# Expert-weight loads issued from a GpSimd copy beside the first row gather, the first rows turned three steps later, and eight weight subtractions on GpSimd

## The chip, the cores and the metric

One core of one Trainium2 chip runs the whole program. The metric is the device time of one execution in microseconds (us), as the median of several executions. The engines are TensorE (PE: matmul and transpose), VectorE (DVE), ScalarE (ACT), GpSimd (POOL) and SyncE (SP, which here only issues transfers). Each runs its own instructions in their order, and they wait for each other by semaphores.

## The reference

Three stages follow each other: attention within clusters, a dense feed-forward layer (FFN), and a layer of eight experts with one chosen expert per token.

```python
x = attention(q, k, v, centroids)                 # (1536 tokens, 512)
h = np.maximum(x @ w_in, 0.0)                     # 512 x 2048
x = h * h @ w_out                                 # 2048 x 512
do_compute = x @ w_skip > 0
e_idx = np.argmax(x[do_compute] @ w_gate, axis=1) # 8 experts
out = x.copy()
for e in range(8):
    mask = e_idx == e
    h = np.maximum(xc[mask] @ w1[e], 0.0)         # 512 x 1024
    y[mask] = gate_w[mask, None] * (h @ w2[e])    # 1024 x 512
out[do_compute] = xc + y
```

All data are fp32. The change lies where the FFN hands over to the experts.

## The kernel before

Every fp32 product is made of three matmuls on a split of each operand: a high part (names that end in `h`, fp32r, rounded by a cast on ACT) and a low part (names that end in `l`, the difference, subtracted on DVE or GpSimd).

**The FFN** works on four chunks of 384 tokens in four passes over the hidden width; its last matmuls add into `acc` (L1087), and `x` of a block of 128 tokens is complete when DVE has added the last pass (L1095). Each block is then stored twice, to the scratch `xd` (L815) and to the output `out` (L816); the last chunk's stores go out on ACT's queue. `turn_x` transposes it too (L819, copied by ACT to `xs`, L821) for the routing products `lps` (L825).

**The routing** counts how many tokens want each expert, gives each its rank within its expert, and makes lists of rows. The fullest expert gets two lists: A, its first 128 tokens, which can be known before the last chunk is routed, and B, the next ones; the other seven experts have one each. `choose()` finds the fullest expert and writes its number and that of the next to `pi`. `place(n)` reads expert numbers from `pi` into registers of SP, and `fetch()` issues the loads of weights: pieces of 512 KB, as many as there are free staging buffers (five at first: three `st` and two of the `xc` tiles that aren't needed any more), and again whenever one comes free. `half_weights` consumes a piece: ACT casts it (`wih`, `woh`, L761), two subtractions of 128x512 make the low part (`wil`, `wol`, L765). The tables `ENG0` to `ENG2` say on which engines, `a` for ACT, `v` for DVE and `p` for GpSimd, with eight entries for the eight pieces of an expert (four of w1, four of w2); `ENG1` is for the second expert in the order.

**The expert units** are numbered u = 0 to 8: units 0 and 1 are lists A and B with the weights of the fullest expert, unit u from 2 on is expert u - 1 in the order. `gather(u)` fetches the rows of a list with an indirect transfer from GpSimd's queue (L1017), the first one from `out`, the others from `xd`. `parts()` transposes the rows (`xps`, L1025), ACT casts them (`xh`, or `hh` for the hidden values, L1028), DVE subtracts (`xl`, `hl`, L1029). `g1` makes the hidden products `hps`, `g2` the products `acc` (both L1035), `turn_h` transposes the hidden values, and `finish` scales the rows, adds them (`yo`, L1056) and scatters them to `out` (L1058). `between(gen, f)` runs `f` behind the second of the four groups of three matmuls of a product, so that the transposes and what follows on ACT and DVE lie beside the rest.

**The order.** The last steps of the FFN and unit 0 form one stream of steps on TensorE, `base()`. At the step numbers of the table `EVENTS` other work is put in: `e` the next part of the routing up to the third chunk (`early()`), `l` that of the last chunk (`late()`), `c` one piece of expert weights, `x` the transposes of list A (`x_of_A`). TensorE's order in this stretch is written by hand in that way; on ACT, DVE and GpSimd a scheduler orders the instructions by priority and readiness, and each engine then runs its list strictly in order. Behind the stream comes a loop over the units 1 to 8.

Of the kernel before, what the change touches and what calls it, by code (L numbers as in the profile page):

```python
# [7 lines left out]
F32 = mybir.dt.float32  # L8
F32R = mybir.dt.float32r
BF16 = mybir.dt.bfloat16  # L10
I32 = mybir.dt.int32
AF = mybir.ActivationFunctionType
ALU = mybir.AluOpType
# [23 lines left out]
PE, ACT, DVE, POOL, SP = (mybir.EngineType.PE, mybir.EngineType.Activation, mybir.EngineType.DVE,  # L37
                          mybir.EngineType.Pool, mybir.EngineType.SP)
EVENTS = ((1, 'e'), (2, 'e'), (3, 'e'), (4, 'e'), (8, 'e'), (11, 'e'), (12, 'c'), (13, 'e'), (15, 'c'),
          (16, 'cce'), (18, 'el'), (21, 'x'), (22, 'lcc'), (25, 'c'), (26, 'l'), (28, 'lc'), (30, 'l'), (34, 'll'))  # L40
ENG0 = ('av',) * 8
ENG1 = ('av',) * 8
ENG2 = ('av',) * 8
HOLD = 2
M0 = {DVE, PE, ACT, POOL}
AFTER = 0
PACE = 3
# [5 lines left out]
def clustered_attention_moe(  # L53
# [16 lines left out]
    nc = tc.nc  # L70
# [4 lines left out]
    E, _, F2 = w1.shape  # L75
# [24 lines left out]
    inner = ExitStack()  # L100
    inner.enter_context(tc.manual_schedule(engines=M0))
    nc.vector.memset(slot, 1.0)
# [30 lines left out]
    def do(gen):  # L133
        for _ in gen:
            pass
# [130 lines left out]
    with ExitStack() as actx:  # L266
# [417 lines left out]
        for i in range(-LA, NQ + GT + 1):  # L684
            if i == CLOSE:
                inner.close()
            for op in ORDER.split():
                op, lag = op.rstrip("'"), op.count("'")
# [13 lines left out]
    rp = ctx.enter_context(tc.tile_pool(name="rp", bufs=1, reuse_waits="tile"))  # L702
# [24 lines left out]
    loads = [h + (c,) for h in halves for c in (0, 2)]  # L727
    ENGS = [ENG0, ENG1] + [ENG2] * E

# [5 lines left out]
    def stage(t):  # L735
        free.append(t[:, 0:1024].rearrange("p (c f) -> p c f", c=2))

    def fetch():

        while free and loads and loads[0][0] < len(e_reg):  # L740
            p, kind, n, c = loads.pop(0)
            st = free.pop(0)
            nc.sync.dma_start(out=st, in_=w_slice(e_reg[p], kind, n)[:, c:c + 2])
            loaded.append(st)
# [39 lines left out]
    def econvert_to(units):  # L784
        while edone[0] < min(units, len(halves)):
            if next(egen) == "unit":
                edone[0] += 1
# [16 lines left out]
    ixp, pi = [rp.tile([128, E], I32, name=nm) for nm in ("ixp", "pi")]  # L804
# [97 lines left out]
    def ranks(ch, base=None):  # L902

        sbs = [128, GT, 128]
        rk = rank[:, ch * GT:ch * GT + GT]
        if base is not None:
            rkb = rp.tile([128, GT, 1], F32, name="rkb", bufs=2)
            nc.vector.tensor_scalar(out=rkb, in0=rk, scalar1=base, scalar2=None, op0=ALU.subtract)
            rk = rkb
        so = rp.tile(sbs, BF16, name="so", bufs=2)  # L910
        nc.vector.tensor_tensor(out=so, in0=slot.rearrange("p (o s) -> p o s", o=1).to_broadcast(sbs),
                                in1=rk.to_broadcast(sbs), op=ALU.is_equal)
        return so

    def slots(ch, sum, so):

        sl = ps_l.tile([128, 5, E], F32, name="sl", tag="l")
        for i in range(GT):
            nc.tensor.matmul(out=sl.rearrange("p a e -> p (a e)"), lhsT=so[:, i],
                             rhs=pay[:, ch * GT + i].rearrange("p a e -> p (a e)"),  # L920
                             start=(i == 0), stop=(i == GT - 1))
        if ch == 0:
            nc.vector.tensor_copy(out=sum[:, 0:5], in_=sl)
        else:
            nc.vector.tensor_tensor(out=sum[:, 0:5], in0=sl, in1=sum[:, 0:5], op=ALU.add)
# [7 lines left out]
    def choose():  # L933

        nc.vector.tensor_reduce(out=cmax, in_=cnt, op=ALU.max, axis=AX.X)
        nc.vector.tensor_scalar(out=full, in0=cnt, scalar1=cmax, scalar2=None, op0=ALU.is_equal)
        nc.vector.tensor_tensor(out=full, in0=full, in1=rev8[:, 0], op=ALU.mult)
        er = rp.tile([128, 1], F32, name="er")
        nc.vector.tensor_reduce(out=er, in_=full, op=ALU.max, axis=AX.X)
        nc.vector.tensor_scalar(out=full, in0=full, scalar1=er, scalar2=None, op0=ALU.is_equal)  # L940
        nc.vector.tensor_scalar(out=pi[:, 0:1], in0=er, scalar1=-1.0, scalar2=float(E), op0=ALU.mult, op1=ALU.add)
        nc.vector.tensor_scalar(out=pi[:, 1:2], in0=full[:, 1:2], scalar1=-1.0, scalar2=1.0,
                                op0=ALU.mult, op1=ALU.add)
        nc.vector.tensor_scalar_min(nA, cmax, 128.0)
        place(2)

    def place(n):
        while len(e_reg) < n:
            p = len(e_reg)
            e_reg.append(nc.sync.value_load(pi[0:1, p:p + 1], min_val=0, max_val=E - 1))  # L950
            if p == 0:
                fetch()

    def pick(i, sum):

        nc.vector.tensor_tensor(out=t2[:, 0:5], in0=sum[:, 0:5], in1=fullb[:, 0:5], op=ALU.mult)
        nc.vector.tensor_reduce(out=sAB[i][:, 0:5], in_=t2[:, 0:5], op=ALU.add, axis=AX.X)
        index(ixAB[i], sAB[i][:, 5:6], sAB[i].rearrange("p (a e) -> p a e", e=1))
        lists[i] = (ixAB[i], sAB[i][:, 5:6])

    def early():

        for ch in range(NC - 1):
            while done[0] <= ch:
                yield
            yield from route(ch)
            so = ranks(ch)
            yield
            if ch == NC - 2:
                choose()  # L970
            slots(ch, sg, so)
            if ch == NC - 2:
                pick(0, sg)
                gather(0)
            if ch < HOLD:
                stage(xc[ch])
            if ch == NC - 2:
                so = ranks(0, nA)
            yield
        for ch in range(NC - 1):  # L980
            slots(ch, sgB, so)
            if ch < NC - 2:
                so = ranks(ch + 1, nA)
            yield

    def late():
        yield from route(NC - 1)
        so, so2 = ranks(NC - 1, nA), ranks(NC - 1)
        yield
        slots(NC - 1, sgB, so)  # L990
        pick(1, sgB)
        gather(1)
        for ch in range(HOLD, NC):
            stage(xc[ch])
        yield
        slots(NC - 1, sg, so2)
        nc.vector.tensor_tensor(out=sgp, in0=sg[:, :, 0:1].to_broadcast([128, 6, E]), in1=sg, op=ALU.subtract)
        nc.vector.tensor_tensor(out=sgp, in0=sgp, in1=fullb, op=ALU.mult)
        nc.vector.tensor_tensor(out=sgp, in0=sgp, in1=sg, op=ALU.add)
        index(ixp, gp, sgp)  # L1000
        for p in range(1, E):
            lists[p + 1] = (ixp[:, p:p + 1], gp[:, p:p + 1])
        gather(2)
        nc.vector.tensor_copy(out=pi, in_=sgp[:, 5])
        place(E)
        yield


    UN = E + 1
# [3 lines left out]
    def gather(u):  # L1013

        xg = xgs[u % 3]
        nc.gpsimd.memset(xg, 0.0)
        nc.gpsimd.indirect_dma_start(  # L1017
            out=xg, in_=xd if u else out, in_offset=bass.IndirectOffsetOnAxis(ap=lists[u][0], axis=0),
            out_offset=None, bounds_check=N - 1, oob_is_err=False)

    def parts(src, name):

        tps = ps_x.tile([128, 4, 128], F32, name="xps", tag="x")
        for c in range(4):
            nc.tensor.transpose(out=tps[:, c], in_=src[:, c * 128:(c + 1) * 128], identity=ident)  # L1025
        hh = ep.tile([128, 4, 128], F32R, name=name + "h")
        hl = ep.tile([128, 4, 128], F32R, name=name + "l")
        nc.scalar.copy(out=hh, in_=tps)  # L1028
        nc.vector.tensor_tensor(out=hl, in0=tps, in1=hh.bitcast(F32), op=ALU.subtract)  # L1029
        return hh, hl  # L1030

    def products(ps, x, w, start, stop):
# [13 lines left out]
    def turn_h(u, n):  # L1046
        hp_t[u, n] = parts(hs_t.pop((u, n)), "h")

    def g2(u, n):
        if n == 0:  # L1050
            y_t[u] = ps_o.tile([128, DM], F32, name="acc")
        yield from products(y_t[u], hp_t.pop((u, n)), hexp[max(u - 1, 0), 1, n], n == 0, n == FB - 1)
# [45 lines left out]

    LG = 2
    bg = early()  # L1100
    lead = len(steps) - NF
    s2 = 0
# [40 lines left out]
    def between(gen, f):  # L1143
        for i, _ in enumerate(gen):
            if i == 1:
                f()
            yield
# [8 lines left out]
    n = 0  # L1156
# [22 lines left out]
    for u in range(1, UN):  # L1179
        econvert_to(4 * u)  # L1180
        do(g1(u, 0))
        if u > 1:
            do(g2(u - 1, 1))
            finish(u - 1)
            turn_h(u, 0)
        if u + 2 < UN:
            gather(u + 2)
        econvert_to(4 * u + 2)
        do(g1(u, 1) if u > 1 else between(g1(u, 1), lambda: turn_h(u, 0)))
        if u + 1 < UN:  # L1190
            xp_t[u + 1] = parts(xgs[(u + 1) % 3], "x")
        do(g2(u, 0))
        turn_h(u, 1)
    do(g2(UN - 1, 1))
    finish(UN - 1)

# [65 lines left out]
```

## Time and profile before

| what | us |
|---|---|
| median of 3 executions | 688.0 (686.8 to 688.48) |
| the profiled execution | 688.21 |
| its span, first to last instruction | 686.5 |
| TensorE busy | 655.3 (95%) |
| VectorE busy | 481.0 (70%) |
| ScalarE busy | 415.1 (60%) |
| GpSimd busy | 253.0 (37%) |
| mean granted TensorE clock | 0.984 of full |

The span leaves 1.7 us of the profiled execution outside. Times in rows count from the start of the span. The FFN ends near 555 us, routing and unit 0 lie between 540 and 575, and from there to 678 TensorE works through the units 1 to 8. A busy share is a mean over all stages, so the stretch around the change is read by itself, in rows in order of time.

### The profile page before, as it was taken

To read this page: it belongs to the slowest core of one execution; us is meant where nothing else is said; L and a number is where in the kernel's file an instruction comes from. 1 tells how busy PE (TensorE), PEld (TensorE's weight loads), DVE (VectorE), ACT (ScalarE), POOL (GpSimd) and SP (SyncE) were. 2 spreads that over 40 slices of the span, in tenths; PEclk is the share of its full clock that TensorE was granted. 3 is DMA by queue.
4 is the path that set the end of the run, shared out by engine and by line. 5 is a ranking of instruction groups with operands and counts; after the bars stand their busy time and mean duration, and the time that the engine had idled before them with its cause. 6 is when DMAs were issued, how large, how long until landed. Compare 5 with 4: busy or idle time off the path is not lost. (4 is left out here: it accounts for less than half of the span.)

```text
span 686.5 us, 11273 instructions
## 1 busy us (share of the span) xinstructions
PE 655.3 (95%) x3769; PEld 569.2 (83%) x3769; DVE 481.0 (70%) x928; ACT 415.1 (60%) x846; POOL 253.0 (37%) x329
## 2 busy tenths in 40 slices
PE   7889999999999999899999999999999898999994
PEld 6688988988888888889899999999888676888883
DVE  5678999999999999664365656522244688899950
ACT  6779989989998986444433333322232275778830
POOL 4534555536365445644344453421110203113110
PEclk9999999999999999999999999999999989999998
DMA  6567565655655200213212222101222596999900
GB/s 138 144 163 198 136 160 134 149 139 137 149 122 126 55 13 1 69 62 103 67 63 77 69 71 91 40 0 47 93 91 82 177 336 243 369 361 362 364 14 23
DMA packets 72034, 89.90 MB, mean 131 GB/s; under 512 B 32384, under 2 KB 43584, under 8 KB 71968
## 3 DMA queue, kind: packets, MB, share of 16 engines
q1 hardware_dynamic: 69664, 84.52, 41.7%
q0 software_dynamic: 1440, 3.01, 1.2%
q10 hardware_dynamic: 864, 1.57, 0.6%
q8 instruction: 32, 0.52, 0.3%
q14 instruction: 34, 0.28, 0.1%
HBM read 62.18 MB, written 9.44 MB: 104 GB/s over the span
## 5 line engine op out<-in xcount | busy, mean ns | idle before, releaser
L580 DVE TENSOR_TENSOR pl<-pt,ph 128x384 fp32r<-128x384 f32 x192 | 103.5, 550 | 19.8 <-ACT ph L571 18.3
L259 ACT ACTIVATE r<-hps 128x384 f32<-128x384 f32 x62 | 30.4, 491 | 125.8 <-PE hps L252 120.6
L557 PE MATMUL pt<-ident,p 128*128 128x128 f32 x576 | 97.1, 279 | 4.7 <-DVE pl L580 3.7
L515 PE MATMUL sc<-B,A 80*128 80x384 f32 (+1 forms) x384 | 93.4, 364 | 4.5 <-DMA A<-hi 1.8
L571 ACT CAST ph<-pt 128x384 fp32r<-128x384 f32 x192 | 89.7, 480 | 10.5 <-PE pt L557 9.7
L522 DVE TENSOR_REDUCE nm<-sc 128x1 f32<-128x768 f32 x96 | 90.9, 947 | 3.5 <-PE sc L515 3.4
L262 DVE TENSOR_TENSOR hl<-r,hh 128x384 fp32r<-128x384 f32 x62 | 37.4, 604 | 77.0 <-POOL hh L138 77.0
L531 ACT ACTIVATE p<-sc,nm 128x768 f32<-128x768 f32 x96 | 87.3, 909 | 6.0 <-DVE nm L522 5.5
L557 PEld LDWEIGHTS pt<-ident,p 128*128 128x128 f32 x576 | 70.8, 142 | 20.2 <-DVE pl L580 13.1
L138 POOL TENSOR_SCALAR hh<-r 128x384 fp32r<-128x384 f32 x62 | 36.5, 589 | 137.9 <-ACT r L260 118.8
L1087 PE MATMUL acc<-woh,hh 128*128 128x512 f32 x186 | 74.6, 401 | 0.0
L1087 PE MATMUL acc<-woh,hl 128*128 128x512 f32 x186 | 73.9, 397 | 0.0
L1087 PE MATMUL acc<-wol,hh 128*128 128x512 f32 x186 | 73.9, 397 | 0.0
L590 PE MATMUL av<-ph,vs 128*128 128x384 f32 x192 | 73.4, 382 | 0.1
L515 PEld LDWEIGHTS sc<-B,A 80*128 80x128 f32 (+1 forms) x384 | 63.9, 193 | 9.6 <-ACT p L531 5.3
L590 PE MATMUL av<-pl,vs 128*128 128x384 f32 x192 | 65.7, 342 | 0.6 <-DVE pl L580 0.6
L252 PE MATMUL hps<-A,wil 128*128 128x384 f32 x184 | 62.1, 338 | 1.8 <-POOL wil L184 1.8
L252 PE MATMUL hps<-A,wih 128*128 128x384 f32 x184 | 62.5, 340 | 0.0
L252 PE MATMUL hps<-B,wih 128*128 128x384 f32 x184 | 62.1, 337 | 0.0
L1087 PEld LDWEIGHTS acc<-woh,hl 128*128 128x128 f32 x186 | 35.3, 190 | 8.0
L1087 PEld LDWEIGHTS acc<-woh,hh 128*128 128x128 f32 x186 | 35.2, 190 | 5.8 <-DVE xc L1095 0.2
L1087 PEld LDWEIGHTS acc<-wol,hh 128*128 128x128 f32 x186 | 35.3, 190 | 5.3
(260 smaller groups left out, 1474.6 us busy)
## 6 DMA issues: line engine op xcount, KB each, us to landing
xc<-in_moe_w_dram SPq DMA_DIRECT2D x34, 512.0 KB, 5.8
st<-in_moe_w_dram SPq DMA_DIRECT2D x30, 512.0 KB, 5.7
st<-in_moe_w_in_dram SPq DMA_DIRECT2D x64, 128.0 KB, 2.9
st<-in_moe_w_out_dram SPq DMA_DIRECT2D x16, 512.0 KB, 3.5
A<-hi SPq DMA_DIRECT2D x30, 192.0 KB, 3.1
B<-hi SPq DMA_DIRECT2D x30, 192.0 KB, 3.1
qn<-in_q_dram SPq DMA_DIRECT2D x16, 192.0 KB, 3.3
kn<-in_k_dram SPq DMA_DIRECT2D x16, 192.0 KB, 3.6
```

The source lines that it names most:

```text
L138: nc.gpsimd.tensor_scalar(out=o, in0=i, scalar1=1.0, scalar2=0.0, op0=ALU.mult, op1=ALU.add)
L252: nc.tensor.matmul(out=hps, lhsT=wi[w][:, c, f * 128:(f + 1) * 128], rhs=xhl[ch][a][:, c], start=(n == 0), stop=(n == 3 * KD - 1))
L259: nc.scalar.activation(out=r, in_=hps, func=AF.Relu)
L262: nc.vector.tensor_tensor(out=hl, in0=r, in1=hh.bitcast(F32), op=ALU.subtract)
L515: nc.tensor.matmul(out=sc[:, c, 0:384], lhsT=A[h][0:kk, a, t * 128:(t + 1) * 128], rhs=Bk[h][0:kk, a, c * 384:(c + 1) * 384], start=(a == ...
L522: nc.vector.tensor_reduce(out=nm_t[i], in_=sc_t[i][:, :, 0:384], op=ALU.max, axis=AX.XY, negate=True)
L531: nc.scalar.activation(out=p, in_=sc[:, :, 0:384], func=AF.Exp, bias=nm, scale=1.0, accum_out=su_t[n, c][:, t, h:h + 1])
L557: nc.tensor.transpose(out=pt[:, c], in_=p_t[i][:, n, c * 128:(c + 1) * 128], identity=ident)
L571: nc.scalar.copy(out=block(i, n)[by_pool].bitcast(F32) if by_pool else block(i, n)[0], in_=pt_t[i, n])
L580: nc.vector.tensor_tensor(out=pl, in0=pt_t.pop((i, n)), in1=ph.bitcast(F32), op=ALU.subtract)
L590: nc.tensor.matmul(out=av, lhsT=vs[:, c, 2 * h:2 * h + 2].rearrange("p x d -> p (x d)"), rhs=r[:, c], start=(c == 0 and i == 0), stop=(c = ...
L1087: nc.tensor.matmul(out=acc, lhsT=h2[a][:, i * 128:(i + 1) * 128], rhs=wo[w][:, f], start=(f == 0 and n == 0), stop=(f == NF - 1 and n == 2))
```

## The change

Five edits:

- The event `x` (transposes of list A) moves from step 21 to step 24.
- The first four pieces (w1) of the second expert in the order have their low parts subtracted on GpSimd instead of DVE: eight instructions of 128x512.
- `choose()` no longer calls `place(2)`. Behind `gather(0)` in the program's text a GpSimd copy of two numbers, `first2`, is made, and `place` reads from that, so that SP's first register load, and behind it the first five weight loads, wait for this copy.
- In `parts()` the cast and the subtraction get a higher priority in the scheduler (`AHEAD`).
- In the last unit the transposes of the second half of the hidden values are put between the groups of the first half's product, as units 0 and 1 have it already.

```diff
-          (16, 'cce'), (18, 'el'), (21, 'x'), (22, 'lcc'), (25, 'c'), (26, 'l'), (28, 'lc'), (30, 'l'), (34, 'll'))
+          (16, 'cce'), (18, 'el'), (22, 'lcc'), (24, 'x'), (25, 'c'), (26, 'l'), (28, 'lc'), (30, 'l'), (34, 'll'))
-ENG1 = ('av',) * 8
+ENG1 = ('ap',) * 4 + ('av',) * 4
+AHEAD = 120
...
         nc.vector.tensor_scalar_min(nA, cmax, 128.0)
-        place(2)
-
-    def place(n):
+
+    def place(n, pi):
...
                 gather(0)
+
+                first2 = rp.tile([128, 2], I32, name="first2")
+                nc.gpsimd.tensor_copy(out=first2, in_=pi[:, 0:2])
+                place(2, first2)
...
-        place(E)
+        place(E, pi)
...
-        nc.scalar.copy(out=hh, in_=tps)
-        nc.vector.tensor_tensor(out=hl, in0=tps, in1=hh.bitcast(F32), op=ALU.subtract)
+        with tc.high_priority(offset=AHEAD):
+            nc.scalar.copy(out=hh, in_=tps)
+            nc.vector.tensor_tensor(out=hl, in0=tps, in1=hh.bitcast(F32), op=ALU.subtract)
...
-        do(g2(u, 0))
-        turn_h(u, 1)
+        if u + 1 < UN:
+            do(g2(u, 0))
+            turn_h(u, 1)
+        else:
+            do(between(g2(u, 0), lambda: turn_h(u, 1)))
```

The lines of the changed kernel are one to eight numbers higher: the gather is L1021, the copy L977, the subtractions L766, the casts L762, the out store L817, `xs` L822, `parts()` L1029 and L1033, the products L1040.

GpSimd, from the FFN's last high parts `hh` to the gathers of list A (index `ixA`), list B (`ixB`) and unit 2 (`ixp`). Before:

```order
L138 TENSOR_SCALAR hh<-r 128x384 x21
L1017 DMA u<-out_dram,ixA 128x512
L1017 DMA u<-xd,ixB 128x512
L1017 DMA l_5821<-xd,ixp 128x512
L1058 DMA out_dram<-yo,ixA 1536x512
```

With the change:

```order
L139 TENSOR_SCALAR hh<-r 128x384 x20
L977 COPY first_6541<-pi 128x2
L139 TENSOR_SCALAR hh<-r 128x384
L1021 DMA u<-out_dram,ixA 128x512
L766 TENSOR_TENSOR wil<-xc_91,wih 128x512 x2
L766 TENSOR_TENSOR wil<-xc_92,wih 128x512 x2
L766 TENSOR_TENSOR wil<-st,wih 128x512 x4
L1021 DMA u<-xd,ixB 128x512
L1021 DMA l_5821<-xd,ixp 128x512
```

The copy stands ahead of the gather of list A, with one `hh` between them, and the eight subtractions stand ahead of the gather of list B.

ACT, from the last chunk's first stores to the first cast of `woh` (`xc_94` are blocks of `x`; `xh` is the cast of list A). Before:

```order
L815 DMA xd<-xc_94 128x512
L761 CAST wih<-st 128x1024
L816 DMA out_dram<-xc_94 128x512
L761 CAST wih<-st 128x1024
L821 COPY xs<-xps 128x512
L761 CAST wih<-st 128x1024
L1028 CAST xh<-xps 128x512
L761 CAST wih<-xc_91 128x1024
L815 DMA xd<-xc_94 128x512
L816 DMA out_dram<-xc_94 128x512
L821 COPY xs<-xps 128x512
L761 CAST woh<-xc_92 128x1024
```

With the change:

```order
L816 DMA xd<-xc_94 128x512
L817 DMA out_dram<-xc_94 128x512
L762 CAST wih<-st 128x1024 x2
L822 COPY xs<-xps 128x512
L816 DMA xd<-xc_94 128x512
L762 CAST wih<-st 128x1024
L762 CAST wih<-xc_91 128x1024
L1033 CAST xh<-xps 128x512
L817 DMA out_dram<-xc_94 128x512
L822 COPY xs<-xps 128x512
L762 CAST woh<-xc_92 128x1024
```

The first cast of weights has moved behind the first store to `out`, the copy `xs` stands behind two casts as it did, and `xh` behind four.

TensorE, from the FFN's last products to the first hidden product of unit 0. Before:

```order
L1087 MATMUL acc<-woh,hl 128x512
L1025 MATMUL xps<-ident,u 128x128 x4
L1087 MATMUL acc<-woh,hh 128x512
L1087 MATMUL acc<-wol,hh 128x512
L1087 MATMUL acc<-woh,hl 128x512
L819 MATMUL xps<-ident,xc_94 128x128 x4
L825 MATMUL lps<-wgs,xs 128x9 x4
```

With the change:

```order
L1092 MATMUL acc<-woh,hl 128x512
L820 MATMUL xps<-ident,xc_94 128x128 x4
L826 MATMUL lps<-wgs,xs 128x9 x4
L1092 MATMUL acc<-woh,hh 128x512
L1092 MATMUL acc<-wol,hh 128x512
L1092 MATMUL acc<-woh,hl 128x512
L1092 MATMUL acc<-woh,hh 128x512
L1092 MATMUL acc<-wol,hh 128x512
L1092 MATMUL acc<-woh,hl 128x512
L1029 MATMUL xps<-ident,u 128x128 x4
L1040 MATMUL hps<-wih,xh 128x512
```

The transposes of list A (`u`) have moved behind the routing's transposes, its products and the last six products of the FFN, and stand now right ahead of unit 0.

## Rows read from the trace of the kernel before

**Rows 1.** Stretches: us; busy (instructions) of PE, PEld, DVE, ACT, POOL; PEclk; DMA share; GB/s.

```profile
545.50:548.20 2.70, 0.09 (x2) 0.01 (x1) 0.50 (x1) 0.00 (x0) 0.00 (x0) 1.00 1.00 369
548.20:555.40 7.20, 7.01 (x26) 5.67 (x27) 4.39 (x7) 6.29 (x8) 0.00 (x0) 0.55 1.03 385
...
566.00:569.30 3.30, 1.64 (x13) 1.11 (x13) 3.30 (x12) 2.46 (x4) 0.00 (x0) 1.00 0.91 325
569.30:572.70 3.40, 3.40 (x9) 2.62 (x9) 3.40 (x16) 2.59 (x4) 2.30 (x2) 0.51 0.56 203
...
577.00:673.50 96.50, 96.38 (x461) 78.44 (x462) 81.07 (x138) 66.12 (x86) 17.59 (x20) 1.00 0.79 286
```

**Rows 2.** TensorE's waits from 530 to 686 us: total, times, longest.

```profile
PE xps L1025 <- DMA u<-out_dram,ixA: 2.6, 1, 2.6
PE sl L919 <- DVE pay L896: 1.7, 2, 1.1
```

**Rows 3.** In order of time, SP: start, us, instruction, count.

```profile
539.51 1.66 SPq L743 DMA_DIRECT2D st<-in_moe_w_dram  x3
541.41 0.98 SPq L743 DMA_DIRECT2D xc<-in_moe_w_dram  x2
545.53 0.38 SPq L743 DMA_DIRECT2D st<-in_moe_w_dram  x1
```

**Rows 4.** In order of time, GpSimd: in brackets the idle time before and its releaser.

```profile
540.58 1.56 POOL L1017 DMA_INDIRECT u<-out_dram,ixA  x1 [0.62 <-DVE hl L262]
570.09 1.38 POOL L1017 DMA_INDIRECT u<-xd,ixB  x1 [27.95 <-DMA xc<-in_moe_w_dram]
```

**Rows 5.** The tile ixA (gather 0 and a later scatter).

```profile
DMA to landing us min/median/max: 7.6/7.7/7.8
```

**Rows 6.** The tile ixB (gather 1 and a later scatter).

```profile
DMA to landing us min/median/max: 3.6/4.2/4.9
```

**Rows 7.** In order of time, DVE, routing of the last chunk.

```profile
562.96 0.69 DVE L765 TENSOR_TENSOR wil<-xc,wih 128x512 fp32r<-128x512 f32 x1
...
569.66 0.15 DVE L929 SCALAR_TENSOR_TENSOR ixB<-sB 128x1 int32<-128x1 f32 x1
```

**Rows 8.** In order of time, TensorE, from gather 0 to list B.

```profile
551.08 1.71 PE L825 MATMUL lps<-wgs,xs 128*128 128x9 f32 x8
...
555.35 0.58 PE L1035 MATMUL hps<-wih,xh 128*128 128x512 f32 x1
...
574.62 0.60 PE L1025 MATMUL xps<-ident,u 128*128 128x128 f32 x4
```

**Rows 9.** In order of time, TensorE, the last two units.

```profile
661.25 0.60 PE L1025 MATMUL xps<-ident,hs 128*128 128x128 f32 x4
661.60 0.48 PE L1035 MATMUL hps<-wih,xh 128*128 128x512 f32 x1
...
673.27 0.60 PE L1025 MATMUL xps<-ident,hs 128*128 128x128 f32 x4
674.54 0.51 PE L1035 MATMUL acc<-woh,hh 128*128 128x512 f32 x1 [0.68 <-ACT hh L1028]
...
675.27 0.50 PE L1035 MATMUL acc<-woh,hl 128*128 128x512 f32 x1
```

**Rows 10.** In order of time, ACT.

```profile
543.03 1.05 ACT L761 CAST wih<-st 128x1024 fp32r<-128x1024 f32 x1 [3.66 <-DMA st<-in_moe_w_dram]
...
548.59 1.05 ACT L761 CAST wih<-st 128x1024 fp32r<-128x1024 f32 x1 [4.51 <-DMA u<-out_dram,ixA]
549.54 0.58 ACT L821 COPY xs<-xps 128x512 f32<-128x512 f32 x1
...
561.40 1.03 ACT L761 CAST wih<-xc 128x1024 fp32r<-128x1024 f32 x1
```

**Rows 11.** Line 184, GpSimd: count, duration ns min/median/max, first and last start.

```profile
L184 POOL TENSOR_TENSOR wil<-u,wih x16: 1277/1390/1715, 102.1 to 436.4; 128x512 fp32r<-128x512 f32 x16
L184 POOL TENSOR_TENSOR wol<-u,woh x16: 1273/1296/1607, 131.6 to 446.4; 128x512 fp32r<-128x512 f32 x16
```

## The prediction

> **What bounds the kernel now.** I read the page, a table of stretches, TensorE's waits, and the instructions in order of time. The page gives TensorE 95% of the span (the table above has its busy time); from 577.00 to 673.50 us it is busy 96.38 of 96.50 us at full clock [rows 1], so a microsecond gained or lost in front of 577 reaches the end. What can still move lies where the FFN hands over to the expert units, and behind 673.5. Three places:
>
> First, gather 0 (list A): issued at 540.58, landed 7.6 us later, and TensorE waits 2.6 us for it [rows 2, 4, 5]. After that stop the clock is 0.55 over 7.20 us [rows 1], which costs 7.20 x 0.45 = 3.2 us of matmul time. The five 512 KB weight loads that SP issued from 539.51 on are in flight beside it [rows 3], and DMA is full [rows 1]; their being the reason of the 7.6 us is an inference.
>
> Second, routing. From 566.00 to 569.30 TensorE works 1.64 of 3.30 us, mostly waiting for DVE's `pay` (1.7 us of the waits), then runs 3.40 us at clock 0.51, a loss of 1.7 us [rows 1, 2]. Gather 1 (list B) goes out at 570.09, 0.4 us after its index, on a GpSimd that had been idle for 27.95 us, and its rows land 3.6 us later [rows 4, 6, 7] (the larger figures of rows 6 and 7 belong to a later scatter with the same index; 570.09 + 4.9 would be past its reader). B's transposes start at 574.62 with no wait before them [rows 8]: gather 1 has under 1 us of slack (570.09 + 3.6 = 573.7).
>
> Third, the last unit: transposes at 673.27, the first matmul on their result at 674.54, another wait at 675.27 [rows 9].
>
> **The change, part by part.**
>
> *The loads.* By its words the change asks for them behind the first gather. The order shows otherwise: SP's register load waits for the GpSimd copy, and that copy stands ahead of gather 0. So the loads move by a copy and a semaphore; I estimate 0.3 to 0.4 us, about the spacing of small DVE rows and one wait; bounds 0 to 1 us. Gather 0 keeps its place behind the same last `hh`, and still meets five loads. I leave its landing at 548.1.
>
> *Transposes of A three acc groups later.* TensorE may now run three matmuls and four transposes before it meets anything late. But ACT's first weight cast stands behind an out store that waits for gather 0 (that is where the 4.51 us idle of the row at 548.59 comes from [rows 10]); in the old order one cast (543.03 [rows 10]) came before that store, in the new none, and the copy `xs` stands behind two casts. So 548.1 + 0.4 (store) + 2 x 1.05 + 0.6 (the copy [rows 10]) = 551.2: TensorE, done with its three matmuls and the transposes at about 546.7, waits about 4.4 us for `xs`, and `lps` starts where it did, 551.08 [rows 8]. The stall isn't removed, its releaser changes. Behind it stand 8 `lps`, 6 acc matmuls at half clock, 4 transposes and the cast `xh`: 551.2 + 1.7 + 2.6 + 0.7 + 0.8 = 557.0 against 555.35 for the first `hps` [rows 8]. That is +1.7 us on TensorE's stream. The first store's staging buffer comes free later too: the load that went out at 545.53 [rows 3] needs that first cast and its subtractions, so goes at about 551. The weights of expert 1 follow, and the cast at 561.40 [rows 10] moves to about 563.3 (+1.9; bounds -4, if gather 0 lands early, and +3).
>
> *Eight subtractions from DVE to GpSimd.* DVE is relieved of 8 x 0.6 = 4.8 us (0.69 each, overlapping) from 562.96 on [rows 7], in the stretch where `pay` and the index of B are made; I take 2 us off B's index (569.66 to about 567.7), bounds 0 and 4.8. But the order puts all eight ahead of gather 1 on GpSimd, which works in order. This program has the same form there already, 128x512 fp32r from fp32: median 1390 and 1296 ns, smallest 1273 [rows 11]. So 8 x 1.30 to 1.39 = 10.4 to 11.1 us from the end of the first cast, 563.3 + 1.05 = 564.4. They pace themselves: a cast gives two, 2.6 us, and the casts come faster than that. End 574.8 to 575.5. Gather 1 goes out at about 575.2 and not at 570.09: **+5.1 us**. The landing is bounded by 3.6 us, its own row, and 7.6, gather 0 with loads beside it [rows 5, 6]; I take 4.2, near its own row, with a little for the loads of the next experts that may now be in flight. B's transposes start at 579.4 for 574.62: **+4.8** (bounds 574.8 + 3.6 and 575.5 + 7.6, +3.8 and +8.5). TensorE's +1.7 from above lies beside this wait: its part of unit 0 would end between 573 and 576.3, and it then stands idle for 3 to 6 us.
>
> *The clock after that idle.* The stretches show two such stops [rows 1, 2]: 2.61 us idle, then 7.20 us at 0.55 (loss 3.2); half busy over 3.30 us, then 3.40 us at 0.51 (loss 1.7). I take **+2.4** between them; lower bound 0.
>
> *The last unit.* The transposes of the second half move in between. Inside the stream this handover takes 661.60 - 661.25 = 0.35 us, here 1.27 [rows 9]: -0.92. The matmul at 675.27 comes 0.73 behind the one at 674.54, with one between them; two steps in the stream take some 0.4 (461 instructions in 96.38 us [rows 1]), so its wait is up to 0.3; I take 0.2. Together **-1.1 us**, bounds -1.3 and -0.9; scatter and what follows don't change.
>
> *The rest.* AHEAD moves the `hh` cast and `hl` up in the scheduler; in the units TensorE loses nothing there that could be won (96.38 of 96.50 us busy [rows 1]), and I count nothing. Expert weights: from 577 on TensorE never waits for them; a later start of TensorE gives them more room. If their cover were gone it would show as waits of `hps` or `acc` for `wil`, `wol`.
>
> Sum: 4.8 + 2.4 - 1.1 = +6.1 us. Against the profiled execution, 688.21 us for a span of 686.5, that is 694.3; it stands 0.2 us above the median of 688.0, so **694.1 us**. By bounds (3.8 + 0 - 1.3 and 8.5 + 3.2 - 0.9 on 688.0) this case goes from 690.5 to 698.8.
>
> **Rivals.**
>
> *Slower still (699.6 us).* GpSimd's and DVE's subtractions hold each other up: both read two operands. For it: the GpSimd rows spread from 1273 to 1715 ns [rows 11], and DVE has `wol` subtractions and routing to do then. Against: the medians stay near the bottom. If each of the eight waits for one DVE subtraction (0.69 us [rows 7]), gather 1 leaves 5.5 us later: 694.1 + 5.5 = 699.6. It decides when the eight rows average over 1.7 us. [...]
>
> *No change (688.8 us).* The weights of expert 1 arrive as before (first cast ends 562.45), GpSimd is done 10.4 later at 572.9, gather 1 lands at 576.5: +1.9, and TensorE, 1.7 us late itself, hardly stops, so its clock stays: +1.9 - 1.1 = +0.8 on 688.0. For it: the cast at 561.40 had no idle before it that a load would have ended [rows 10]. It needs `xs` at 551 not to push the buffers back.
>
> *Faster (685.2 us).* One mechanism: gather 0 lands 3.6 us after its issue, as gather 1 does [rows 6], at 544.2, since the loads start later. Then the store doesn't wait, neither `xs` nor TensorE stops at 546.7, the clock stays, and everything is some 4 us early: first cast of expert 1 ends at 558.4, eight subtractions end at 569.2 (10.8 later), the index is there (567.7), B is ready at 572.9 for 574.62: -1.7, and -1.1 at the tail. It decides if gather 0 lands before 545.5. Against: the loads start a third of a microsecond later, still before the gather's 540.58, and five of them, 2.6 MB at the 369 GB/s of that stretch [rows 1], take 7 us.
>
> That the change doesn't do what it says (the loads not being behind the gather) is part of the forecast; the rival just told is what it would be if it did.
>
> **How the numbers follow.** Forecast 0.60, slower still 0.13, no change 0.15, faster 0.12. About 0.3% (2.1 us; 685.9 to 690.1) is what a measurement of this kernel can tell from no change. Forecast and slower rival lie above: 0.73; no change 0.15; faster 0.12. Likeliest time 694.1; the forecast's own range is 690.5 to 698.8. The range that holds 8 in 10 leaves out the faster case and a part of the slowest: 687.5 to 699.0.
>
> **What would show it.** Right: GpSimd's eight `wil` rows of 1.3 us in a row with gather 1 behind them at about 575; TensorE waiting for `u<-xd,ixB` some 3 to 6 us and a clock near 0.5 behind that; TensorE waiting for `xs` and no more for gather 0, some 4 us; first `hps` near 557; transposes of the last unit followed by an acc matmul within 0.4 us. Wrong: gather 0 landing before 546, rows of GpSimd under 0.9 us or over 1.7, gather 1 out before 572, or a wait in the units behind 580 where there was none.

## The result, and the profile after

The changed kernel takes 697.6 us (median of 4 executions, 696.69 to 698.14) against 687.51 us for the kernel before (4 executions): a ratio of 1.014, 95% interval 1.0123 to 1.0157, so 8.5 to 10.8 us more. The forecast was 694.1 us, +6.1. Its profiled execution has a span of 695.5 us against 686.5. One execution of c2_all (below) ran at a granted clock of 0.556 and took 1061 us; its ratio leaves it out.

The table sets the landmarks of both traces against the issue of gather 0 (540.58 and 540.17 us), since what lies ahead of it differs a little from one execution to the next.

| us behind the issue of gather 0 | before | changed | more |
|---|---|---|---|
| first hidden product of unit 0 | 14.77 | 17.56 | 2.8 |
| first routing row of DVE, last chunk (`mx`) | 20.05 | 23.32 | 3.3 |
| index of list B (`ixB`) | 29.08 | 37.85 | 8.8 |
| transposes of list B | 34.04 | 43.11 | 9.1 |
| last scatter | 138.35 | 145.34 | 7.0 |
| end of the span | 145.92 | 155.33 | 9.4 |

So 3.3 us are lost in front of the routing, 5.5 in it, 2.1 are won between list B and the last scatter, and 2.4 are lost behind that.

GpSimd in order of time, the answer to [rows 4] (start, duration, instruction; in brackets the idle time before and its releaser):

```profile
538.58 0.18 POOL L977 COPY first<-pi 128x2 int32<-128x2 int32 x1 [1.83 <-DVE pi L943]
...
540.17 1.56 POOL L1021 DMA_INDIRECT u<-out_dram,ixA  x1 [0.64 <-DVE hl L263]
565.39 2.48 POOL L766 TENSOR_TENSOR wil<-xc,wih 128x512 fp32r<-128x512 f32 x2 [23.66 <-PE xps L1029]
568.28 2.53 POOL L766 TENSOR_TENSOR wil<-xc,wih 128x512 fp32r<-128x512 f32 x2 [0.41 <-ACT wih L762]
570.76 5.66 POOL L766 TENSOR_TENSOR wil<-st,wih 128x512 fp32r<-128x512 f32 x4
578.45 1.02 POOL L1021 DMA_INDIRECT u<-xd,ixB  x1 [2.02 <-DVE ixB L930]
```

The eight subtractions last 1.25 to 1.30 us each, but for two beside the rows of `so` below (1.58 and 1.65), and end at 576.4. Gather 1 leaves two microseconds later, and its releaser is the index, not GpSimd's own queue. The index comes from DVE; its rows beside the subtractions, in order of time, the answer to [rows 7]:

```profile
565.43 1.25 DVE L867 TENSOR_TENSOR oh<-oh,mr 128x24 f32<-128x24 f32 x1
566.61 0.17 DVE L889 TENSOR_REDUCE gate<-ex 128x3 f32<-128x24 f32 x1
566.72 1.19 DVE L870 TENSOR_TENSOR oh<-oh,sel 128x24 bf16<-128x24 f32 x1
...
568.33 0.17 DVE L886 TENSOR_TENSOR rke<-rk,oh 128x24 f32<-128x24 f32 x1
...
570.87 1.60 DVE L912 TENSOR_TENSOR so<-slot,rkb 128x384 bf16<-128x384 f32 x1
572.39 1.23 DVE L893 CAST vals<-gate 128x3 bf16<-128x3 f32 x1
573.54 0.55 DVE L912 TENSOR_TENSOR so<-slot,rank 128x384 bf16<-128x384 f32 x1
574.01 1.22 DVE L895 TENSOR_TENSOR gate<-gate,vals 128x3 f32<-128x3 f32 x1
575.26 1.20 DVE L893 CAST vals<-gate 128x3 bf16<-128x3 f32 x1
...
578.02 0.15 DVE L930 SCALAR_TENSOR_TENSOR ixB<-sB 128x1 int32<-128x1 f32 x1
```

An operation on 24 numbers a partition takes 1.2 us, as long as one subtraction of GpSimd; a reduction among them, or one that reads `rk` from PSUM, takes 0.17. The two rows of `so` are one operation on tiles of one size, 1.60 and 0.55 us; the second begins where one subtraction ends and the next has not begun (573.6). TensorE's waits, the answer to [rows 2] (total, times, longest):

```profile
PE lps L826 <- ACT xs L822: 5.3, 1, 5.3
PE sl L920 <- DVE pay L897: 4.3, 2, 3.8
PE rk L874 <- DVE oh L870: 2.6, 1, 2.6
```

The wait for gather 0 is gone and one of twice its length, for `xs`, has come; the waits for the routing have grown from 2.7 us to 7.2 (with one of 0.3 for `sgB`). No wait is for the rows of list B. Of the 9.1 us that list B's transposes are late, 2.8 are the later first hidden product, 4.5 the longer waits for the routing, and some 1.7 a stretch at half clock that the kernel before does not have (0.50 over 3.3 us from 568.0 on, behind the stop for `oh`). The reason of the wait for `xs` is on ACT, as in [rows 10], where the store to `out` waits for gather 0. Of the tile `ixA` the larger figure is gather 0's, 8.4 us for 7.6 before, so it landed at 548.6:

```profile
DMA to landing us min/median/max: 7.5/8.0/8.4
```

```profile
548.62 0.37 ACTq L817 DMA_DIRECT2D out_dram<-xc  x1
549.04 1.04 ACT L762 CAST wih<-st 128x1024 fp32r<-128x1024 f32 x1 [10.16 <-DMA xd<-xc]
...
549.99 1.04 ACT L762 CAST wih<-st 128x1024 fp32r<-128x1024 f32 x1
550.93 0.58 ACT L822 COPY xs<-xps 128x512 f32<-128x512 f32 x1
```

ACT stands idle for 10 us, and `xs` comes behind two casts; in the kernel before the first cast ran at 543.03, ahead of the store, and only one stood between the store and `xs` [rows 10]. TensorE in order of time, the answer to [rows 8] and [rows 9]:

```profile
551.56 1.88 PE L826 MATMUL lps<-wgs,xs 128*128 128x9 f32 x8 [5.31 <-ACT xs L822]
...
557.73 0.50 PE L1040 MATMUL hps<-wih,xh 128*128 128x512 f32 x1 [0.68 <-ACT xh L1033]
...
583.28 0.60 PE L1029 MATMUL xps<-ident,u 128*128 128x128 f32 x4
...
679.65 0.60 PE L1029 MATMUL xps<-ident,hs 128*128 128x128 f32 x4
680.00 0.48 PE L1040 MATMUL acc<-woh,hh 128*128 128x512 f32 x1
```

In the last unit the first matmul behind the transposes comes 0.35 us behind them instead of 1.27. Behind the last scatter nothing computes. Over the whole span the page of the changed kernel has one transfer of instructions more than the 34 of the kernel before:

```profile
q14 instruction: 35, 0.29, 0.1%
```

### The profile page after: what moved, and what is told of

Read it like the earlier page. It is cut to its first block, busy times and chain, and to the rows that moved or that the text cites. A ratio compares the mean times of both kernels' runs of the same rounds, so it can differ in the third digit from the quotient of the medians.

```text
span 695.5 us, 11283 instructions
## 1 busy us (share of the span) xinstructions
PE 655.2 (94%) x3769; PEld 570.1 (82%) x3769; DVE 483.3 (69%) x920; ACT 415.3 (60%) x846; POOL 262.7 (38%) x338
```

## The experiments

The changed kernel's ratio is the one above, to 687.51 us; every other is to the kernel before in the same sitting and on the same chip (688.8, 689.0 and 688.9 us in three sittings). So 0.001 is 0.7 us. Landmarks are from the profiles, in us behind the issue of gather 0:

| kernel | ratio (95%) | first hidden | `mx` | `mx` to `ixB` | list B | scatter to end |
|---|---|---|---|---|---|---|
| before | 1 | 14.77 | 20.05 | 9.03 | 34.04 | 7.57 |
| changed | 1.0140 (1.0123 to 1.0157) | 17.56 | 23.32 | 14.53 | 43.11 | 9.99 |
| a1_dve_subs | 1.0032 (1.0012 to 1.0053) | 17.07 | 24.19 | 9.26 | 37.50 | 7.60 |
| b1_subs | 1.0110 (1.0057 to 1.0164) | 13.68 | 18.91 | 14.82 | 38.02 | 10.02 |
| d_memset | 0.9979 (0.9954 to 1.0004) | 15.50 | 20.67 | 7.97 | 32.73 | 7.69 |
| b5_p2 | 1.0007 (0.9988 to 1.0027) | 14.57 | 19.83 | 9.03 | 33.81 | 7.49 |
| b3_first2 | 1.0029 (1.0008 to 1.0050) | 15.78 | 21.72 | 9.03 | 35.74 | 7.53 |
| b4_behind | 1.0087 (1.0052 to 1.0121) | 10.70 | 20.51 | 12.65 | 36.89 | 7.65 |
| b8_split | 0.9984 (0.9959 to 1.0010) | 9.45 | 18.42 | 10.09 | 33.49 | 7.63 |
| b7_latex | 1.0106 (1.0072 to 1.0140) | 15.84 | 28.12 | 13.41 | 45.50 | 7.58 |
| a3_latex_ahead | 0.9998 (0.9981 to 1.0015) | 15.94 | 21.40 | 10.98 | 37.34 | 7.55 |
| c3_xs | 1.0013 (0.9990 to 1.0035) | 11.40 | 21.95 | 11.77 | 38.34 | 7.66 |
| c2_all | 0.9973 (0.9952 to 0.9994) | 11.21 | 18.34 | 10.97 | 34.27 | 7.69 |
| b2_tail | 0.9963 (0.9938 to 0.9989) | 13.66 | 19.05 | 9.54 | 33.56 | 7.71 |

**The subtractions.** From the changed kernel (a1) they are taken back, to the kernel before (b1) they alone are added.

```diff
-ENG1 = ('ap',) * 4 + ('av',) * 4
+ENG1 = ('av',) * 8
```

> The changed kernel with its eight subtractions for the second expert back on DVE, all else as changed. Theory L (DVE instructions with two operands in SBUF stand still while a GpSimd subtraction runs): the small routing rows of DVE go back from about 1.2 us to 0.2 us, the index of list B comes some 5.5 us earlier, and the time falls from 697.6 to about 691.5 us (what is left is the 2.9 us that the front lost, with the tail's gain against it). Rival G (list B's gather is late because it is queued behind the subtractions on GpSimd): about 692 to 693 us, since DVE has its 4.8 us of subtractions back. Rival S (the scheduler's new order on DVE and ACT is what costs): stays within 1 us of 697.6, and the small rows of DVE stay long.

> The kernel before with only the eight subtractions moved to GpSimd. Theory L: small routing rows of DVE with two operands in SBUF last about 1.2 us, those with one operand in PSUM, or reductions, stay at 0.2; index of B about 5.5 us later than 569.66; time 687.5 + 5.5 = about 693 us. Rival G: DVE's rows stay at 0.2 us, the index is ready before 569.7 and the gather leaves when the last subtraction ends, at about 573: 687.5 + 3 = 690.5 us. Rival S: no change from 687.5, within 1 us.

a1 comes to 1.0032: of the change's 10 us some 7.4 are the subtractions'. b1 alone costs 1.1%, 7.6 us (3.9 to 11.3). In both, 2.4 us of this lie behind the last scatter (**The end**, below). In both pairs the way from `mx` to the index is 5.3 to 5.8 us longer with them, and theory L stands; G falls, for in b1 GpSimd ended its last one at 570.8 and gather 1 left at 573.45. In a1 the same DVE rows are short again:

```profile
567.85 0.17 DVE L867 TENSOR_TENSOR oh<-oh,mr 128x24 f32<-128x24 f32 x1
...
568.06 0.18 DVE L870 TENSOR_TENSOR oh<-oh,sel 128x24 bf16<-128x24 f32 x1
...
571.97 0.55 DVE L912 TENSOR_TENSOR so<-slot,rkb 128x384 bf16<-128x384 f32 x1
```

**As much GpSimd work, but fills.** In place of each subtraction a copy of one column and two fills with zeros; the kernel leaves out the low part of this expert's w1:

```diff
             for i in range(2):
+                if p == 1 and kind == 0 and src is None:
+                    nc.gpsimd.tensor_copy(out=lo[:, c + i, 0:1], in_=hi.bitcast(F32)[:, c + i, 0:1])
+                    nc.gpsimd.memset(lo[:, c + i].bitcast(F32), 0.0)
+                    nc.gpsimd.memset(lo[:, c + i].bitcast(F32), 0.0)
+                    continue
...
```

> The kernel before, where GpSimd, in place of each of the eight subtractions that the change gives it, copies one column of the high part and fills the low part with zeros, twice (two fills of 0.55 us and a small copy, about as long as a subtraction; the low part of this expert's w1 is left out). GpSimd is as busy as in the change, behind the same casts, but reads next to nothing. [...] Rival (any GpSimd work of that length stops DVE): rows of 0.6 to 1.2 us, 14 us from the first routing row to the index, and about 693 us.

The routing takes 7.97 us, a microsecond less than before, so GpSimd's being busy is not what stops DVE, and the rival falls. DVE in order of time, beside fills that run from 563.7 to 570:

```profile
563.71 0.18 DVE L874 TENSOR_TENSOR oh<-oh,sel 128x24 bf16<-128x24 f32 x1
563.81 0.42 DVE L894 TENSOR_SCALAR gate<-gate 128x3 f32<-128x3 f32 x1
...
565.18 0.48 DVE L897 CAST vals<-gate 128x3 bf16<-128x3 f32 x1
...
565.77 0.55 DVE L916 TENSOR_TENSOR so<-slot,rkb 128x384 bf16<-128x384 f32 x1
566.24 0.61 DVE L897 CAST vals<-gate 128x3 bf16<-128x3 f32 x1
```

The rows that read two tensors keep the time they have in the kernel before (0.18 us for `oh`, 0.55 for `so`); the casts and the row with one input, 0.16 us there, take up to 0.61 (a fill lasts 0.5). So a subtraction and a fill hold up different rows: beside a subtraction in the changed kernel rows with two SBUF inputs and casts take 1.2 us, a reduction and a row with a PSUM input 0.17; beside a fill casts and rows of TENSOR_SCALAR lose up to 0.45 us, and no row of two tensors more than 0.06. Why the two differ no run shows.

**The same eight subtractions elsewhere**, for the third expert, behind the routing:

```diff
-    ENGS = [ENG0, ENG1] + [ENG2] * E
+    ENGS = [ENG0, ENG1, ('ap',) * 4 + ('av',) * 4] + [ENG2] * E
```

> The kernel before with eight subtractions moved to GpSimd as in the change, but those of the third expert in the order, which fall behind the routing. Theory (the price is that of the routing's short DVE instructions in a row, each held up by one subtraction, with TensorE waiting for their end): DVE's subtractions beside them get longer, TensorE doesn't wait for it, and the ratio to before is 1.000 within 0.003. Rival (GpSimd's subtractions cost wherever they stand, by delaying a gather or the weights): ratio 1.005 or more and a wait of TensorE for wil or for rows of a list.

As expected: 1.0007. GpSimd's six in a row and DVE's three beside them (0.68 us each otherwise):

```profile
583.94 8.48 POOL L765 TENSOR_TENSOR wil<-st,wih 128x512 fp32r<-128x512 f32 x6
```

```profile
590.06 3.50 DVE L765 TENSOR_TENSOR wol<-xc,woh 128x512 fp32r<-128x512 f32 x3
```

Here both sides lose (GpSimd's longest takes 1752 ns, DVE's 1787), and TensorE waits for none of it. It is the place, a chain of some 20 short DVE rows that TensorE waits for, that makes the price of the routing.

**The end.** Behind the last scatter all kernels have 7.5 to 7.7 us, but the changed one and b1 have 10.0. These two alone have 35 in the row of instruction transfers. `ENG1` also serves the block for leftover rows, which is in the program and skipped: its calls of `half_weights` are made with the number 1, so with the new table that block holds 64 more instructions for GpSimd. The traces narrow it down: in all fourteen the span ends 2.7 to 3.0 us behind the start of the last transfer of instructions, and that one starts 4.6 to 4.9 us behind the last scatter in twelve kernels and 7.1 us behind it in these two. So the 2.4 us are those of one later transfer; that the longer block is what makes it needed is what fits, and no run changes the block alone.

**The loads.** The copy alone (b3), and the loads really behind the gather (b4: the copy reads a value made from the gather's index):

```diff
                 gather(0)
...
+                pz = rp.tile([128, 1], I32, name="pz")
+                pq = rp.tile([128, 2], I32, name="pq")
+                nc.vector.tensor_scalar(out=pz, in0=ixAB[0], scalar1=0.0, scalar2=None, op0=ALU.mult)
+                nc.vector.tensor_tensor(out=pq, in0=pi[:, 0:2], in1=pz.to_broadcast([128, 2]), op=ALU.add)
+                nc.gpsimd.tensor_copy(out=first2, in_=pq)
+                place(2, first2)
```

> The kernel before with only the copy on GpSimd and the loads that wait for it (the copy stands ahead of gather 0 here too). If the loads that stay ahead of the gather are what keeps it 7.6 us: gather 0 still lands at about 548, ACT's first cast is behind the store that waits for it, and the time is 687.5 to 689.5 us. If 0.3 us of delay are enough for the gather to go first: it lands before 545.5 and the time is about 683.5 us.

> The kernel before with the loads really behind gather 0: the copy reads a value made from the gather's index, and stands behind the gather on GpSimd. Theory (the five loads ahead of it are why gather 0 takes 7.6 us): it lands in about 4 us, near 544.5; TensorE's 2.6 us wait for it and the half clock behind it go, the loads start about 2 us later, and the time falls by 3 to 5 us, to about 683.5 us. Rival (the 7.6 us have another cause, such as the stores and the first use of the queue): it lands at 548 as before, the loads are 2 us later, and the time is 688 to 690 us.

In b3 gather 0 lands 7.6 us after its issue, as expected, and the loss is 2 us (0.6 to 3.4), at the upper end of what was expected. a1 and a3 (below) differ by this copy alone; there it costs 2.3 us. The rows show how: in the three kernels with this copy (changed, a1, b3) ACT's first cast of weights stands behind the store that waits for gather 0 (in b3 it starts at 550.15, after 9.36 us idle); in the kernel before and in a3 it stands ahead of it (543.03 [rows 10] and 542.22). So `xs` comes a cast later, and behind TensorE's stop b3 has a clock of 0.52 over 10.3 us where the kernel before has 0.55 over 7.2 [rows 1]. In b4, where the loads start 2.9 us behind the gather, the tile's landing is what the theory said, 4.0 us for the gather and 3.6 for the scatter with the same index:

```profile
DMA to landing us min/median/max: 3.6/3.8/4.0
```

So the five loads are why it took 7.6 us. TensorE no longer waits for it, and its first hidden product comes 4 us earlier. Yet the kernel is 6 us slower: the loads start 3.9 us later, and ACT and DVE pay. ACT has `xh` and the next `xs` behind casts that wait for loads (TensorE waits 1.9 us for `xh`), and DVE has 13 weight subtractions between `mx` and the index where before had 7: 6 x 0.6 = 3.6 us, which is the 12.65 against 9.03 of the table. TensorE now waits there:

```profile
PE rk L873 <- DVE oh L869: 3.9, 1, 3.9
```

The forecast of 683.5 left this out. With two loads in front and three behind (b8) the waits nearly balance:

```diff
+    early2 = [2]
...
-        while free and loads and loads[0][0] < len(e_reg):
+        while free and loads and loads[0][0] < len(e_reg) and len(loaded) < early2[0]:
...
                 gather(0)
...
+                for t in free:
+                    nc.gpsimd.tensor_copy(out=t[:, 0, 0:1], in_=pz)
+                early2[0] = 99
+                fetch()
```

> The kernel before, with the first two of the five loads asked for at the same place as before and the other three behind gather 0 (GpSimd writes one column of their buffers behind the gather). Theory: gather 0 has two loads ahead of it, not five; it lands in 4 to 5 us, TensorE's 2.6 us wait and the half clock behind it go or shrink, and ACT still has its first two pieces early, so that no copy for the routing stands behind a cast that waits for a load; 3 us off the front, of which the weights of unit 0 (loads three to five 1.5 us later) leave 1 to 2: 685.5 to 687 us. Rival (a weight load delayed is paid in full by the routing on ACT and DVE, as with all five behind the gather): 689 to 692 us.

Gather 0 lands after 4.7 us, the first hidden product comes 5.3 us earlier, list B half a microsecond; the time is not clear of no change.

**List A's transposes.** Alone (b7), with the priority and the tail but without subtractions and copy (a3), and with `xs` given priority too (c3), where ACT makes it ahead of the waiting store:

```diff
-        nc.scalar.copy(out=xs_t[T], in_=xps)
+        with tc.high_priority(offset=200):
+            nc.scalar.copy(out=xs_t[T], in_=xps)
```

> The kernel before with only the transposes of list A at step 24. TensorE has three more matmuls and the routing's transposes ahead of its first wait, and one cast stays ahead of the store here. Theory: xs comes at about 551 as before, TensorE waits 4 us for it and not 2.6 us for the gather, the first hidden product starts 1.5 to 2 us later; 688.5 to 690.5 us. Rival (the 2.6 us wait is hidden by the later place): 685 us.

> The kernel before with the transposes of list A at step 24, the scheduler's priority for the casts and subtractions of parts(), and the last unit's transposes put in between: the change without its subtractions on GpSimd and without its copy for the loads. Theory (late transposes alone cost 7 us because DVE has eight weight subtractions ahead of xl, which the priority mends): TensorE's wait of 2.8 us for xl and the 20 us at half clock behind it are gone; what stays is the wait of about 4 us for xs in place of 2.6 us for the gather; with the tail's 1.1 us the ratio to before is 0.998 to 1.003. Rival (the late place itself costs): ratio 1.008 or more.

> The kernel before with list A's transposes at step 24, the priority for parts() and for the copy xs, and the last unit's transposes in between: ACT now makes xs ahead of the store that waits for gather 0. Theory (in the change TensorE still stops for gather 0, through the store on ACT's queue): TensorE meets no wait longer than 1 us between 545 and 552, its clock stays at full, the first hidden product starts about 3.5 us earlier than before, and the ratio to before is 0.992 to 0.996. Rival (the weights of unit 0 or the routing on DVE then set the pace): a wait of TensorE for wil or for the routing takes its place, ratio 0.997 to 1.000.

b7 costs 7.3 us where 1 to 3 were expected. The reason is in DVE's order: `xl` is behind weight subtractions, TensorE stops a second time,

```profile
560.16 0.79 PE L1035 MATMUL hps<-wih,xl 128*128 128x512 f32 x1 [2.82 <-DVE xl L1029]
```

and behind this stop the clock is at half a second time, 0.50 from 559 to 573 us, after 0.50 from 549 to 556 behind the first (the "20 us" of a3's expectation are these two together). With the priority (a3) that wait is 0.2 us, and the ratio 0.9998. So the later place needs AHEAD, and the two with the tail come out even; AHEAD alone was not run. In c3 the wait for `xs` is gone (`mx` should have gained), but ACT then has the store, a cast, another `xs` and a cast ahead of `xh`:

```profile
549.15 0.38 ACTq L817 DMA_DIRECT2D out_dram<-xc  x1
549.57 1.04 ACT L762 CAST wih<-st 128x1024 fp32r<-128x1024 f32 x1 [3.42 <-DMA st<-in_moe_w_dram]
550.52 0.58 ACT L823 COPY xs<-xps 128x512 f32<-128x512 f32 x1
...
551.00 1.05 ACT L762 CAST wih<-xc 128x1024 fp32r<-128x1024 f32 x1
...
551.95 0.59 ACT L1031 CAST xh<-xps 128x512 fp32r<-128x512 f32 x1
```

```profile
552.58 0.60 PE L1038 MATMUL hps<-wih,xh 128*128 128x512 f32 x1 [2.53 <-ACT xh L1031]
```

The stop has moved a second time, and the half clock with it (unit 0's products follow each other every 0.43 us up to 565.6, the FFN's last ones ahead of the stop every 0.23); 0.992 to 0.996 was wrong. c2 adds the split of b8 to c3.

> The same with three of the five first loads behind gather 0 in addition. Theory (gather 0 is no longer on TensorE's path, so its earlier landing frees only the store, and the later loads delay the weights of unit 0): no better than the kernel without that, ratio 0.994 to 0.999. Rival (the store that waits for the gather still holds up ACT's casts): 0.3% better than without.

It is better than c3 by 0.4%, as the rival expectation had it, and its routing starts 3.6 us earlier (18.34 against 21.95); that the earlier landing (5.4 us behind the issue) lets ACT's store go sooner is what fits. At 0.9973, with an interval that ends just below 1, it is faster than both kernels.

**The last unit**, alone:

```diff
-        do(g2(u, 0))
-        turn_h(u, 1)
+        if u + 1 < UN:
+            do(g2(u, 0))
+            turn_h(u, 1)
+        else:
+            do(between(g2(u, 0), lambda: turn_h(u, 1)))
```

> The kernel before with only the last unit's transposes put between the groups of the first half's product. Theory: from the last transposes to the last scatter 1.1 us less; 1.1 us off the time, about 0.16%. Rival (ACT or DVE are late for it at the new place): a new wait of TensorE behind the transposes, and no gain.

0.9963, 0.8 to 4.3 us less. The tail's own share is the 1.1 to 1.2 us expected: from the transposes ahead of it to the last scatter 10.5 us (667.59 to 678.09) against 11.7 (667.23 to 678.93). This one edit is the best of all that ran, with c2; the interval doesn't tell them apart.

## Why the prediction was right or wrong

- **The direction and the range were right**, 697.6 within 687.5 to 699.0, at 10.1 us instead of 6.1. The sum is not confirmed by that, and that it came this near is in part luck: its two largest terms, the queue on GpSimd (+4.8) and the clock behind a stop at list B (+2.4), did not happen, and others that it had at nothing or as a gain came in their place.
- **The loads**: right that gather 0 stays slow (8.4 us to landing; 7.6 in b3). The copy ran at 538.58, ahead of the gather. Measured from the gather's issue the first load moved by 0.7 us, not 0.3 to 0.4 (539.81 for 540.17, before 539.51 for 540.58), so that only one of the five was issued ahead of the gather; it landed late all the same. That loads beside it cause this was called an inference; b4 shows it. What the copy does to ACT's order was counted under the later transposes; a3, which has those without the copy, keeps the cast ahead of the store. The copy's price is 2.0 (b3) to 2.3 us (a1 against a3).
- **TensorE's stop moves to `xs`**: right, 5.3 us for the 4.4 forecast; the first hidden product was 2.8 us late for 1.7. Gather 0 landed 0.8 us later than the forecast's 7.6, so the store went out at 548.6, and `xh` cost another wait of 0.7 us.
- **"I take 2 us off B's index"** is the step that failed. The index was taken to come earlier, DVE being relieved of 4.8 us, with bounds of 0 and 4.8 and no loss; only five of the eight subtractions, 3.0 us, lay between `mx` and the index. It came 5.5 us later from `mx` on: seven short rows each stood behind one GpSimd subtraction for about 1.05 us and an eighth for 0.34, 7.7 us in all, more than the relief. In d_memset, with fills that slow DVE less, the same relief leaves the index 1.1 us earlier from `mx` on.
- **Gather 1 queued behind the subtractions (+4.8)**: their length (1.30 to 1.39 forecast; 1.25 to 1.65 measured, 1.36 on average) and their end (575 forecast, 576.4) were right, but it didn't decide: the index was later still.
- **The slower rival** had the right two engines and the wrong loser. It priced the delay on GpSimd's rows, at one long DVE subtraction each; but six of GpSimd's eight rows kept their pace, two lost 0.3 to 0.4 us, and eight of the routing's short DVE rows waited, seven of them for nearly a whole subtraction. Its deciding point, GpSimd rows over 1.7 us, would not have found it.
- **The clock (+2.4 behind a stop at list B)**: no such stop. TensorE stopped for `oh` and `pay` (2.6 and 3.8 us) ahead of it, and the half clock behind those stops is within the +9.1 us of list B; new in it are the 3.3 us at 0.50 behind `oh`, some 1.7 us.
- **The tail**: right, -1.1 forecast, about -1.2 measured. Another 0.9 us between list B and the last scatter was not forecast; 0.6 of it are two short gaps in unit 1 of the kernel before that the changed one lacks, which the priority may have closed.
- **Left out**: the 2.4 us behind the last scatter. "Scatter and what follows don't change" overlooked that `ENG1` is used by the skipped block too. (Where the prediction says "rows 6 and 7" of the scatter's larger figures, [rows 5] and [rows 6] have them; no sum depends on it.)

Put together in the trace: list B 8.7 us later, counted from the start of the span, -2.1 to the last scatter, +2.4 behind it, +9.0 us of span. Put together by the ratios, taking one edit after the other from the changed kernel (a1, then a3): 7.4 us for the subtractions with the longer end, 2.3 for the copy, and nothing (-0.1) for the later transposes, the priority and the tail together.

## What to carry to other kernels

Before elementwise work goes from VectorE to GpSimd, look at what VectorE does beside it: here short operations with two inputs in SBUF, and casts, in a chain that another engine waits for, seven of eight took about 1.05 us more beside GpSimd subtractions of 1.3 us, while the same move beside long hidden work cost nothing measurable (b5, ratio 1.0007). When a wait on one engine is to be hidden by order, follow every in-order queue behind the late event: here a store on ACT's queue carried gather 0's lateness to `xs`, then to `xh`. An instruction that delays a load can also change the order of what consumes it: the copy of two numbers put a cast behind that store, for 2 us. An option table may also serve code that is skipped.

## What the runs showed of the hardware that was not expected

- Beside a GpSimd subtraction of 128x512 (two SBUF inputs, 1.3 us; changed) DVE operations on 3 to 24 numbers a partition with two SBUF inputs, and casts, last 1.2 us instead of 0.16 unless they begin between two subtractions (0.15 at 570.75 in the changed kernel); reductions and operations with a PSUM input don't change (0.17). Beside GpSimd fills (0.5 us; d_memset) casts and some operations of TENSOR_SCALAR last up to 0.45 us longer, operations on two tensors at most 0.06.
- The indirect gather of 128 rows lands 4.0 us after its issue when the five loads of 512 KB start 2.9 us behind it (b4), 4.7 and 5.4 with two issued ahead and three from 2.1 us behind (b8, c2), and 7.4 to 8.4 in the kernels with all five issued from 1.1 us ahead to 2.2 us behind, even with four of them behind (changed).
- Behind stops of TensorE of nearly one length the clock stayed low for very different times: 0.55 over 7.2 us behind 2.6 us [rows 1], 0.52 over 10.3 behind 2.8 (b3), 0.50 over some 14 behind 2.8 (b7). At half clock those 14 us of b7 are some 7 us of matmul time lost (14 x 0.50), for a stop of 2.8.
